# More places for loaded weights and words, loads later in a queue, evictions on ScalarE, splits one a step

## The chip, the cores and the metric

The kernel runs on one core of a Trainium2 chip. The metric is the device time of one execution in microseconds; the kernel before was timed in three runs.

## The reference

Three layers follow each other. (1) Attention over 2 batches, 8 heads, 768 positions and 64 columns a head, each query seeing 4 sink positions and a window of 128. (2) A mixture of 8 experts over the resulting 1536 x 512 rows: each token takes the best two of noisy logits, and the expert is relu(x w1) w2 with 1024 hidden columns. (3) A dense layer with 2048 hidden columns, whose weights come as float64:

```python
    top2 = np.argpartition(-noisy_logits, 2, axis=1)[:, :2]
    ...
            h = np.maximum(x[mask] @ w1[e], 0.0)
            out[mask] += top2_w[mask, k, None] * (h @ w2[e])
...
    h = x @ w_in
    g = h * (1.0 / (1.0 + np.exp(-h)))
    return (g @ w_out).astype(np.float32)
```

## The kernel before

Every float32 product is made from float16 halves: a high half (ScalarE, a scaled copy or relu) and a low half (VectorE, the value less the high half; `low`, line 126, and `low_relu`, line 131, which also sum what they write). A product is three matmuls: high by high, and twice high by low. The low half of h is needed by the second of the three.

The work runs in three stages: attention (to about 153 us; its end already does a part of expert 0), the experts (`moe`, to about 455 us), the dense layer (`moe2`). Each engine takes its instructions in the order of the program, which is written by hand.

*Experts.* There are 64 steps i = 8e + f (expert e, block f of 128 hidden columns). A step first does `l1(e, f)` (line 995: 12 matmuls over 416 columns, then relu on ScalarE and the low half on VectorE) and then `l2` of the step before (line 1011: 12 matmuls into four PSUM tiles `py`). In expert 0 the first 128 rows are done already, so its matmuls have 288 columns. After that, in this order in a step:

- at f = 0, `y_ev`: the four finished `py` tiles of the expert before are copied to `yT`, two by ScalarE (line 1033), two by VectorE (line 1035);
- `stores`: the store of an output tile evicted a step earlier, on SyncE;
- at f = 2 to 5, `y_pe` transposes a part of `yT` on TensorE (line 1040) and `y_store` copies it from PSUM to a tile `yo`, on ScalarE for even parts (line 1050), on VectorE for odd ones (line 1052);
- `gather`: GpSimd collects the rows of expert e + 2 at f = 5;
- `x_pair` splits gathered rows of the next expert into halves (high, line 974, ScalarE; low, VectorE) in a tile `rows`, and `x_turn` transposes them into `xT` by a transposing DMA on SyncE (line 1351). Both take two of the four parts in a step: in expert 0 splits at f = 3 and 4 and turns at f = 5 and 6, later splits at f = 1 and 2 and turns at f = 3 and 4. Experts alternate between `rows[0]` and `rows[1]`;
- `weights_step(k)`: piece k of the weights is split (high half, line 871, ScalarE; low, VectorE), then SyncE loads piece k + 3 (line 866). Each piece is 512 KB in a place of the pool `wst`, which has three, so that load waits for the low half of piece k. There is one piece a step, and two in a few steps from i = 10 on;
- `decode_step`, five in four steps: the float64 weights of the dense layer become float32 by bit operations, 32 blocks of 128 x 512. An even decode step ends block n - 1 (`a4`: line 939 on VectorE, and either a split into halves, line 945 on ScalarE and a low half on VectorE, for the 16 later blocks, or a store by SyncE, line 950, for the 16 earlier ones), begins block n (`a1`: absolute value of the high words, line 924 on VectorE, then a scaling on GpSimd, line 926) and loads the words of block n + 1 (line 920, two places `f64`). An odd step does two word operations (`a2`, `a3`, lines 930 and 934, VectorE).

*Dense layer.* It begins with the gathers of the y rows of two experts a token (`gather_y`), their weighted sum and their transposes; then ScalarE's queue issues the first three loads of `late` weight pieces, and 48 steps of `l1` (line 1256) and `l2` (line 1273) follow.

Of the kernel before, what the change touches and what calls it, by code (L numbers as in the profile page):

```python
# [8 lines left out]
F32 = mybir.dt.float32  # L9
F32R = mybir.dt.float32r  # L10
F16 = mybir.dt.float16
# [811 lines left out]
class Weights:  # L823


    def __init__(self, ctx, tc, g):
        self.tc, self.g = tc, g
        self.pools = [ctx.enter_context(tc.tile_pool(name="wA", bufs=2))]
        self.stage = ctx.enter_context(tc.tile_pool(name="wst", bufs=3))
        self.u = {}  # L830

    def second(self, ctx):
        self.pools.append(ctx.enter_context(self.tc.tile_pool(name="wB", bufs=2)))
        self.own = ctx.enter_context(self.tc.tile_pool(name="wC", bufs=2))

    def src(self, u, k, h):
        g = self.g
# [18 lines left out]
    def piece(self, u, k, h, late=False):  # L856

        nc = self.tc.nc
        g = self.g
        st = {}  # L860

        def load(eng=nc.sync):
            if u not in self.u:
                self.start(u)
            st["t"] = t = self.stage.tile([128, 2, 512], F32, name="wst")
            eng.dma_start(t, self.src(u, k, h))

        scale = ((SW1, SW2), (SWI, SWO))[u >= 16][k]

        def hi():  # L870
            nc.scalar.activation(self.u[u][k][0][:, 2 * h:2 * h + 2, :], st["t"], AF.Copy, scale=scale)  # L871

        def lo():
            a, b = self.u[u][k]
            low(nc, g, b[:, 2 * h:2 * h + 2, :], st["t"], scale, a[:, 2 * h:2 * h + 2, :])
            if h == 0:
                seen(self.tc, g, a[:, 0, 0:64])

        def scaled(x):
            nc.gpsimd.tensor_scalar(st["t"][:, x], st["t"][:, x], scale, 1.0, op0=OP.mult, op1=OP.mult)  # L880

        def hi_pool(x):
            nc.gpsimd.tensor_scalar(self.u[u][k][0][:, 2 * h + x, :], st["t"][:, x], 1.0, 1.0, op0=OP.mult, op1=OP.mult)

        def lo_pool(x):
            a, b = self.u[u][k]
            nc.gpsimd.tensor_sub(b[:, 2 * h + x, :], st["t"][:, x], a[:, 2 * h + x, :])

        return load, hi, lo, hi_pool, lo_pool, scaled

    def checks(self, u, pool):

        nc = self.tc.nc
        g = self.g
        def total(x, t):
            o = pool.tile([128, 2, 512], F16, name="any", bufs=1)
            nc.scalar.activation(o, t[:, x:x + 2, :], AF.Copy, accum_out=sum_at(g))

        out = [lambda x=x, t=self.u[u][0][1]: total(x, t) for x in (0, 2)]
        return out + [lambda t=self.u[u][k][0]: seen(self.tc, g, t[:, 0, 0:64]) for k in range(2)]  # L900
# [5 lines left out]
def decode(tc, g, pool, W=None):  # L906

    nc = tc.nc
    V = nc.vector
    out = []  # L910
    for q in (2, 3, 0, 1):
        for src, dst in ((g.w_in, g.win_d), (g.w_out, g.wout_d)):
            w = src.bitcast(I32)
            for x in range(4):
                r, c = (128 * x, 512 * q) if dst is g.win_d else (512 * q + 128 * x, 0)
                st = {}

                def load(eng=nc.sync, st=st, w=w, r=r, c=c):
                    st["w"] = t = pool.tile([128, 512, 2], I32, name="f64", bufs=2)
                    eng.dma_start(t, w[r:r + 128, 2 * c:2 * c + 1024].rearrange("p (f w) -> p f w", w=2))  # L920

                def a1(st=st):
                    st["a"] = a = pool.tile([128, 512], F32, name="f32", bufs=2)
                    V.tensor_scalar(a.bitcast(I32), st["w"][:, :, 1], 0x7fffffff, None, op0=OP.bitwise_and)  # L924

                    nc.gpsimd.tensor_scalar(a, a, 2.0 ** -15, 2.0 ** -80, op0=OP.max, op1=OP.mult)  # L926

                def a2(st=st):
                    l = st["w"][:, :, 0]
                    V.tensor_scalar(l, l, 29, -0x80000000, op0=OP.logical_shift_right, op1=OP.bitwise_or)  # L930

                def a3(st=st):
                    l = st["w"][:, :, 0]
                    V.scalar_tensor_tensor(l, st["w"][:, :, 1], -0x80000000, l, op0=OP.bitwise_and,
                                           op1=OP.bitwise_xor)

                def a4(st=st, dst=dst, r=r, c=c, q=q, x=x):
                    a = st["a"].bitcast(I32)
                    V.scalar_tensor_tensor(a, a, 3, st["w"][:, :, 0], op0=OP.logical_shift_left,  # L939
                                           op1=OP.bitwise_xor)  # L940
                    if W and q < 2:
                        k = int(dst is g.wout_d)
                        hi, lo = (t[:, x, :] for t in W.u[16 + q][k])
                        scale = (SWI, SWO)[k]
                        nc.scalar.activation(hi, st["a"], AF.Copy, scale=scale)  # L945
                        low(nc, g, lo, st["a"], scale, hi)
                        if x == 0:
                            seen(tc, g, hi[:, 0:64])
                    else:
                        nc.sync.dma_start(dst[r:r + 128, c:c + 512], st["a"])  # L950

                out.append((load, a1, a2, a3, a4))
    return out


def moe(tc, g, W, wk, ps):
# [72 lines left out]
    def y_ev(e, d):  # L1029
        if d == 0:  # L1030
            yT[e] = wk.tile([128, 4, 512], F32, name="yT", bufs=1)[:, :, :C]
        if d % 2 == 0:
            nc.scalar.activation(yT[e][:, d, part(e)], ys[e][d][:, part(e)], AF.Copy)
        else:
            V.tensor_copy(yT[e][:, d, part(e)], ys[e][d][:, part(e)])

    def y_pe(e, c):
        t = tp[c] = ps.tile([128, 4, 128], F32, name="tpy", tag="PT")
# [6 lines left out]
    def y_store(e, c, src):  # L1045
        t = wk.tile([128, 512], F32, name="yo", bufs=2)
        n = CT[c]
        src = src[:n]
        if c % 2 == 0:
            nc.scalar.activation(t[:n], src, AF.Copy)  # L1050
        else:
            V.tensor_copy(t[:n], src)
        return lambda: nc.sync.dma_start(g.y_d[e * C + c * 128:e * C + c * 128 + n, :], t[:n])
# [45 lines left out]
            loaded[0] += 1  # L1099

    xT[0] = g.xT
    load_ahead(3)
    seq = [(e, f) for e in range(E) for f in range(8)]

    small, stores = [], []
# [1 line left out]
    def weights_step(k):  # L1107
        if k < len(todo):
            todo[k][1]()
            todo[k][2]()  # L1110
            load_ahead(k + 4)

    def decode_step(i):
        n, odd = divmod(i, 2)
        if i > 64:
            return
        if odd:
            dec[n][2]()
            dec[n][3]()
        else:  # L1120
            if n > 0:
                dec[n - 1][4]()
            if n < len(dec):
                dec[n][1]()
                if n + 1 < len(dec):
                    dec[n + 1][0]()

    dstep = [0]
    done = [0]
    for i, (e, f) in enumerate(seq):  # L1130
        l1(e, f)
# [16 lines left out]
        if f == 5 and e + 2 < E:  # L1148
            gather(e + 2)
        if e + 1 < E:  # L1150
            z = 2 * (f - (1 if e else 3))
            for c in (z, z + 1):
                if 0 <= c < 4:
                    x_pair(e + 1, c)
            for c in (z - 4, z - 3):
                if 0 <= c < 4:
                    x_turn(e + 1, c)
        if i == 1:
            small.extend(W.checks(0, wk) + W.checks(1, wk))

# [10 lines left out]
            g.pre()  # L1171
        if i == 7:
            dec[0][0]()
        if i < 9:
            continue
        decode_step(dstep[0])
# [12 lines left out]


def gather_y(tc, g, pool, j, k):
    t = g.yy[j, k] = pool.tile([128, 512], F32, name=("yg", "xg")[k], bufs=4)
    rows = (g.E - 1) * g.C
    if k:
        rows = rows + g.CY if j < 4 else g.E * g.C
    tc.nc.gpsimd.indirect_dma_start(
        out=t, out_offset=None, in_=g.y_d[:rows, :],
        in_offset=bass.IndirectOffsetOnAxis(ap=g.slot[:, j, k:k + 1], axis=0))


def moe2(tc, g, W, wk, ps):
# [92 lines left out]
        x_pe(j, ("M", "PT")[j // 2])  # L1294
        x_ev(j)
    g.rest()
    for p in late[:3]:
        p[0](nc.scalar)
    NQ = g.N // 512
    seq = [(q, f) for q in range(NQ) for f in range(16)]  # L1300
    for i, (q, f) in enumerate(seq):
# [6 lines left out]
        if i < len(late):  # L1308
            late[i][1]()
            late[i][2]()  # L1310
            if i + 3 < len(late):
                late[i + 3][0]()
        if q + 1 < NQ:
            j = 4 * (q + 1)
            for stage, f0 in ((lambda j: (gather_y(tc, g, wk, j, 0), gather_y(tc, g, wk, j, 1)), 2),
# [9 lines left out]
def fast(ctx, tc, g):  # L1325
# [17 lines left out]

    def pair_rows(e, c):

        t = g.rows[e % 2][:, c, :].bitcast(F16)
        return t[:, 0:512], t[:, 512:1024]

    def turn(xT, e, c, n):

        tc.nc.sync.dma_start_transpose(xT[2][:, :, 128 * c:128 * c + n], g.rows[e % 2][:n, c, :].bitcast(F16))

    g.xT_tiles, g.pair_rows, g.turn = xT_tiles, pair_rows, turn
    g.rows = [early.tile([128, 4, 512], F32, name=f"rows{x}") for x in range(2)]
# [67 lines left out]
def general(tc, g):  # L1422
# [4 lines left out]
    with ExitStack() as ctx:  # L1427
# [131 lines left out]
        with ExitStack() as st:  # L1559
            wk = st.enter_context(tc.tile_pool(name="gend", bufs=1))  # L1560
            for stages in decode(tc, g, wk):
                for f in stages:
                    f()

        with ExitStack() as st:
            wk = st.enter_context(tc.tile_pool(name="genc", bufs=1))
# [72 lines left out]
```

## Time and profile before

| | us |
|---|---|
| median of three runs | 722.78 |
| lowest and highest run | 721.03, 723.17 |
| profiled execution, its own time | 721.78 |
| its span in the profile | 720.1 |
| TensorE busy | 668.8 (93%) |
| VectorE busy | 444.0 (62%) |
| ScalarE busy | 313.1 (43%) |
| GpSimd busy | 204.5 (28%) |

The busy shares are means over the three stages, which differ. In the rows below PE is TensorE's matmuls, DVE VectorE, ACT ScalarE, SPq and ACTq the queues in which SyncE and ScalarE issue DMAs. "<-" behind a time in square brackets names what ended an engine's idle time.

### The profile page before, as it was taken

Reading aid. Unit: us, or ns where it says so; the run is one execution under the profiler, and the core shown is the slowest. Engines: PE = TensorE matmul, PEld = TensorE weight load, DVE = VectorE, ACT = ScalarE, POOL = GpSimd, SP = SyncE. Lnnn points to the kernel's source line nnn. Section 1 sums busy time; section 2 is a strip of 40 time slices with the busy share of each in tenths; the row PEclk is TensorE's granted clock in tenths of the full one; section 3 lists DMA queues with packets and bytes.
Section 4 is the critical chain, followed back from the end, with each engine's and each line's share of the span. In section 5 each row is a group of like instructions: output and inputs, shape, how many; then the busy total and the mean of one; then the engine's idle time right before and its main releaser. Section 6 shows DMA issues by size and latency. Waiting matters only on the chain.

```text
span 720.1 us, 11583 instructions
## 1 busy us (share of the span) xinstructions
PE 668.8 (93%) x4292; PEld 373.1 (52%) x4292; DVE 444.0 (62%) x1137; ACT 313.1 (43%) x647; POOL 204.5 (28%) x229
## 2 busy tenths in 40 slices
PE   7999899887888999999999999899999999999994
PEld 4777677455454555555555554344444444444441
DVE  5878888736587879697989863656433343322232
ACT  4887878346544444333545331344222222222221
POOL 5868951122125252434262323231100000000000
PEclk9999999899899999999999999999999999999998
DMA  7876610338598898979595723662311011010001
GB/s 151 198 163 176 178 46 30 118 96 211 177 275 324 224 368 200 340 218 338 180 323 170 203 88 106 180 219 76 85 45 59 1 30 30 5 54 1 1 0 64
DMA packets 111681, 103.49 MB, mean 144 GB/s; under 512 B 77312, under 2 KB 77568, under 8 KB 111616
## 3 DMA queue, kind: packets, MB, share of 16 engines
q1 hardware_dynamic: 106560, 87.72, 42.4%
q0 software_dynamic: 4096, 13.11, 5.8%
q10 hardware_dynamic: 960, 1.84, 0.8%
q8 instruction: 35, 0.57, 0.3%
q14 instruction: 30, 0.25, 0.1%
HBM read 77.29 MB, written 17.30 MB: 131 GB/s over the span
## 4 chain that ended last, share of the span: by engine, by line


## 5 line engine op out<-in xcount | busy, mean ns | idle before, releaser
L995 PE MATMUL ph<-xT,w 128*128 128x416 f16 (+1 forms) x768 | 141.6, 335 | 8.3 <-DMA xT<-rows 6.4
L1011 PE MATMUL py<-h,w 128*128 128x416 f16 (+1 forms) x672 | 126.7, 334 | 12.3 <-DVE h L131 11.7
L1256 PE MATMUL p<-xT,w 128*128 128x512 f16 x576 | 132.1, 379 | 2.1 <-DVE xT L1242 1.4
L1273 PE MATMUL po<-w,h 128*128 128x512 f16 x576 | 132.1, 379 | 0.0
L926 POOL TENSOR_SCALAR f<-f 128x512 f32<-128x512 f32 x32 | 65.0, 2032 | 168.9 <-DVE f L924 161.8
L995 PEld LDWEIGHTS <-w 128*128 128x128 f16 x768 | 75.4, 98 | 60.7 <-DMA xT<-rows 6.6
L1259 DVE TENSOR_TENSOR f<-p,f 128x512 f32<-128x512 f32 x48 | 33.1, 690 | 110.9 <-ACT f L1258 110.9
L1011 PEld LDWEIGHTS <-w 128*128 128x128 f16 x672 | 66.1, 98 | 63.9 <-issue 18.4
L1256 PEld LDWEIGHTS <-w 128*128 128x128 f16 x576 | 56.3, 98 | 70.1 <-issue 2.4
L1273 PEld LDWEIGHTS <-h 128*128 128x128 f16 x576 | 56.2, 98 | 67.8 <-DVE h L126 0.3
L126 DVE SCALAR_TENSOR_TENSOR w<-wst,w 128x1024 f16<-128x1024 f32 x64 | 79.1, 1238 | 15.8 <-ACT w L871 13.4
L1258 ACT ACTIVATE f<-p 128x512 f32<-128x512 f32 x48 | 28.6, 596 | 129.2 <-PE p L1256 127.9
L871 ACT ACTIVATE w<-wst 128x1024 f16<-128x1024 f32 x64 | 66.9, 1047 | 12.0 <-DMA wst<-in_moe_w_dram 12.0
L998 ACT ACTIVATE h<-ph 128x416 f16<-128x416 f32 (+1 forms) x64 | 31.8, 497 | 78.1 <-PE ph L995 75.1
L126 DVE SCALAR_TENSOR_TENSOR h<-f,h 128x512 f16<-128x512 f32 x48 | 33.2, 692 | 33.3 <-ACT h L1261 32.6
L131 DVE SCALAR_TENSOR_TENSOR h<-ph,h 128x416 f16<-128x416 f32 (+1 forms) x64 | 36.3, 566 | 19.9 <-ACT h L998 19.9
L1261 ACT ACTIVATE h<-f 128x512 f16<-128x512 f32 x48 | 30.2, 629 | 37.8 <-DVE f L1259 37.0
L482 ACT ACTIVATE P<-pS,mx 128x260 f32<-128x260 f32 (+1 forms) x96 | 43.0, 458 | 0.5 <-DVE mx L473 0.2
L966 POOL DMA_INDIRECT xg<-x_d,idx x28 | 29.7, 1059 | 23.2 <-DVE topsl L121 13.4
L504 DVE SCALAR_TENSOR_TENSOR plo<-pPT,phi 128x512 f16<-128x512 f32 (+1 forms) x48 | 30.5, 636 | 4.1 <-ACT phi L499 4.1
L945 ACT ACTIVATE w<-f 128x512 f16<-128x512 f32 x16 | 10.1, 630 | 51.7 <-DVE f L939 51.7
L473 DVE TENSOR_REDUCE mx<-pS 128x2 f32<-128x520 f32 (+1 forms) x48 | 31.0, 646 | 1.4 <-PE pS L467 1.2
(252 smaller groups left out, 886.3 us busy)
## 6 DMA issues: line engine op xcount, KB each, us to landing
wst<-in_moe_w_dram SPq DMA_DIRECT2D x64, 512.0 KB
f<-in_moe_w_in_dram SPq DMA_DIRECT2D x16, 512.0 KB
f<-in_moe_w_out_dram SPq DMA_DIRECT2D x16, 512.0 KB
y_d<-yo SPq DMA_DIRECT2D x23, 256.0 KB
rawv<-in_v_dram SPq DMA_DIRECT2D x12, 256.0 KB
x_d<-xs SPq DMA_DIRECT2D x12, 256.0 KB
rows<-in_k_dram SPq DMA_DIRECT2D x11, 256.0 KB
rows<-in_q_dram SPq DMA_DIRECT2D x11, 256.0 KB
```

Of the source, the lines that this page charges most:

```text
L126: nc.vector.scalar_tensor_tensor(o, x, scale, hi, op0=OP.mult, op1=OP.subtract, accum_out=sum_at(g)[:o.shape[0]] if check else None)
L131: nc.vector.scalar_tensor_tensor(o, x, 0.0, hi, op0=OP.max, op1=OP.subtract, accum_out=sum_at(g))
L473: nc.vector.tensor_reduce(t, psS[pr][:, :, :wd], axis=AX.X, op=OP.max, negate=True)
L482: nc.scalar.activation(Pt[n][:, h, :wd], psS[pr][:, a, :wd], AF.Exp, bias=nmx[pr][:, a:a + 1], accum_out=sm[n][:, h:h + 1])
L871: nc.scalar.activation(self.u[u][k][0][:, 2 * h:2 * h + 2, :], st["t"], AF.Copy, scale=scale)
L926: nc.gpsimd.tensor_scalar(a, a, 2.0 ** -15, 2.0 ** -80, op0=OP.max, op1=OP.mult)
L995: nc.tensor.matmul(p[:, v], w[x][:, d, c], xT[e][y][:, d, v], start=d == 0 and k == 0, stop=d == 3 and k == 2)
L998: nc.scalar.activation(hi[:, v], p[:, v], AF.Relu)
L1011: nc.tensor.matmul(ys[e][d][:, v], w[x][:, f % 4, d * 128:(d + 1) * 128], h[y][:, v], start=f == 0 and k == 0, stop=f == 7 and k == 2)
L1256: nc.tensor.matmul(p, w[x][:, d, c], xT[q][y][:, d, :], start=z == 0, stop=z == 11)
L1259: V.tensor_mul(s, p, s)
L1273: nc.tensor.matmul(po[q][t], h[x][:, 128 * t:128 * t + 128], w[y][:, f % 4, :], start=f == 0 and k == 0, stop=f == 15 and k == 2)
```

## The change

- The weight places become five for the pieces from the second expert on: the three of `wst` and two made of `rows[1]`, which is therefore no longer used for split rows: all experts split into `rows[0]`. SyncE loads piece k + 4 after piece k is split; five are loaded ahead instead of three, also at the start of the dense layer, where ScalarE's queue issues them.
- The words have four places `f64`, and an even decode step loads block n + 2. The store of decoded words is issued in the next odd decode step. The first gathered rows of the dense layer take their places among the `f64` tiles.
- The absolute value (`a1`) is an activation Abs of ScalarE that reads the high words as float32.
- All four `y_ev`, and all `y_store` of the experts before the last, are on ScalarE.
- `x_pair` takes one part a step at f = 1 to 4, `x_turn` one at f = 2 to 5, for every expert.
- Scratch output of `checks` goes to `yo` tiles.

```diff
@@ Weights
-        self.stage = ctx.enter_context(tc.tile_pool(name="wst", bufs=3))
+        self.stages = [ctx.enter_context(tc.tile_pool(name="wst", bufs=3))]
+        self.turn = 0
...
-            st["t"] = t = self.stage.tile([128, 2, 512], F32, name="wst")
+            z = self.turn
+            if z < 3:
+                t = self.stages[0].tile([128, 2, 512], F32, name="wst")
+            elif z < 5:
+                t = g.rows[1][:, 2 * z - 6:2 * z - 4, :]
...
+            self.turn = (z + 1) % (3 if u < 2 else 5)
@@ checks
-            o = pool.tile([128, 2, 512], F16, name="any", bufs=1)
+            o = pool.tile([128, 512], F32, name="yo", bufs=2).bitcast(F16)
@@ decode
-                    st["w"] = t = pool.tile([128, 512, 2], I32, name="f64", bufs=2)
+                    st["w"] = t = pool.tile([128, 512, 2], I32, name="f64", bufs=4)
...
-                    V.tensor_scalar(a.bitcast(I32), st["w"][:, :, 1], 0x7fffffff, None, op0=OP.bitwise_and)
+                    nc.scalar.activation(a, st["w"][:, :, 1].bitcast(F32), AF.Abs)
...
-                        nc.sync.dma_start(dst[r:r + 128, c:c + 512], st["a"])
+                        return lambda: nc.sync.dma_start(dst[r:r + 128, c:c + 512], st["a"])
@@ moe
-        if d % 2 == 0:
-            nc.scalar.activation(yT[e][:, d, part(e)], ys[e][d][:, part(e)], AF.Copy)
-        else:
-            V.tensor_copy(yT[e][:, d, part(e)], ys[e][d][:, part(e)])
+        nc.scalar.activation(yT[e][:, d, part(e)], ys[e][d][:, part(e)], AF.Copy)
...
-        if c % 2 == 0:
+        if c % 2 == 0 or e < E - 1:
...
-    load_ahead(3)
+    load_ahead(5)
...
-            load_ahead(k + 4)
+            load_ahead(k + 5)
...
         if odd:
+            while dstore:
+                dstore.pop()()
             dec[n][2]()
             dec[n][3]()
         else:
             if n > 0:
-                dec[n - 1][4]()
+                dstore.extend(f for f in [dec[n - 1][4]()] if f)
             if n < len(dec):
                 dec[n][1]()
-                if n + 1 < len(dec):
-                    dec[n + 1][0]()
+                if n + 2 < len(dec):
+                    dec[n + 2][0]()
...
-            z = 2 * (f - (1 if e else 3))
-            for c in (z, z + 1):
-                if 0 <= c < 4:
-                    x_pair(e + 1, c)
-            for c in (z - 4, z - 3):
-                if 0 <= c < 4:
-                    x_turn(e + 1, c)
+            if 0 <= f - 1 < 4:
+                x_pair(e + 1, f - 1)
+            if 0 <= f - 2 < 4:
+                x_turn(e + 1, f - 2)
...
             dec[0][0]()
+            dec[1][0]()
@@ gather_y
-    t = g.yy[j, k] = pool.tile([128, 512], F32, name=("yg", "xg")[k], bufs=4)
+    if k:
+        t = pool.tile([128, 512], F32, name="xg", bufs=4)
+    else:
+        t = pool.tile([128, 512, 2], I32, name="f64", bufs=4).rearrange("p f w -> p (f w)").bitcast(F32)[:, 0:512]
+    g.yy[j, k] = t
@@ moe2
-    for p in late[:3]:
+    for p in late[:5]:
...
-            if i + 3 < len(late):
-                late[i + 3][0]()
+            if i + 5 < len(late):
+                late[i + 5][0]()
@@ fast
-        t = g.rows[e % 2][:, c, :].bitcast(F16)
+        t = g.rows[0][:, c, :].bitcast(F16)
...
-        tc.nc.sync.dma_start_transpose(xT[2][:, :, 128 * c:128 * c + n], g.rows[e % 2][:n, c, :].bitcast(F16))
+        tc.nc.sync.dma_start_transpose(xT[2][:, :, 128 * c:128 * c + n], g.rows[0][:n, c, :].bitcast(F16))
```

## Rows read from the trace of the kernel before

**Rows 1.** TensorE's waits over the span: line, releaser, us in total, times, longest.
```profile
PE py L1011 <- DVE h L131: 11.7, 12, 2.8
PE ph L995 <- DMA xT<-rows: 6.4, 1, 6.4
```

**Rows 2.** Timeline of TensorE: start us, us, instruction, [idle before].
```profile
182.44 3.72 PE L995 MATMUL ph<-xT,w 128*128 128x416 f16 x12 [6.36 <-DMA xT<-rows]
...
191.69 2.27 PE L995 MATMUL ph<-xT,w 128*128 128x416 f16 x12
...
195.91 2.27 PE L995 MATMUL ph<-xT,w 128*128 128x416 f16 x12
...
200.56 2.27 PE L995 MATMUL ph<-xT,w 128*128 128x416 f16 x12
...
214.56 2.09 PE L1011 MATMUL py<-h,w 128*128 128x416 f16 x11 [1.71 <-DVE h L131]
...
230.26 3.52 PE L1011 MATMUL py<-h,w 128*128 128x416 f16 x11 [2.75 <-DVE h L131]
```

**Rows 3.** Busy us by stretch, experts 3 and 6: length, engines, clock, DMA share, GB/s.
```profile
260.94:298.69 37.75, 35.98 (x209) 20.56 (x208) 29.57 (x69) 15.87 (x24) 14.62 (x10) 1.00 0.93 271
...
374.78:412.15 37.37, 36.15 (x210) 20.55 (x208) 33.35 (x82) 16.57 (x28) 12.44 (x7) 1.00 0.70 213
```

**Rows 4.** VectorE's waits from 337 to 412 us.
```profile
DVE w L126 <- ACT w L945: 7.0, 10, 0.7
```

**Rows 5.** SyncE's queue, its waits from 183 to 440 us.
```profile
SPq L866 <- DVE w L126: 88.8, 25, 7.8
```

**Rows 6.** Groups by line, 187 to 440 us: busy us, mean ns | idle before, releasers.
```profile
L126 DVE SCALAR_TENSOR_TENSOR w<-wst,w 128x1024 f16<-128x1024 f32 x49 | 60.8, 1243 | 6.0 <-ACT w L871 6.0
L871 ACT ACTIVATE w<-wst 128x1024 f16<-128x1024 f32 x49 | 51.3, 1049 | 9.2 <-DMA wst<-in_moe_w_dram 9.2
L131 DVE SCALAR_TENSOR_TENSOR h<-ph,h 128x416 f16<-128x416 f32 x55 | 32.1, 583 | 12.3 <-ACT h L998 12.3
L998 ACT ACTIVATE h<-ph 128x416 f16<-128x416 f32 x54 | 27.5, 510 | 61.2 <-PE ph L995 58.2 <-issue 3.0
L939 DVE SCALAR_TENSOR_TENSOR f<-f,f 128x512 int32<-128x512 int32 x32 | 21.9, 685 | 1.8 <-POOL f L926 1.6
L924 DVE TENSOR_SCALAR f<-f 128x512 int32<-128x512 int32 x32 | 13.5, 423 | 17.9 <-DMA f<-in_moe_w_out_dram 13.1 <-DMA f<-in_moe_w_in_dram 4.9
L945 ACT ACTIVATE w<-f 128x512 f16<-128x512 f32 x16 | 10.1, 630 | 51.7 <-DVE f L939 51.7
L1052 DVE COPY yo<-tpy 128x512 f32<-128x512 f32 (+1 forms) x14 | 9.5, 680 | 0.6 <-PE tpy L1040 0.6
L1050 ACT ACTIVATE yo<-tpy 128x512 f32<-128x512 f32 x13 | 7.7, 594 | 16.7 <-PE tpy L1040 14.3 <-DMA y_d<-yo 2.4
L1035 DVE COPY yT<-py 128x416 f32<-128x416 f32 (+1 forms) x14 | 7.3, 562 | 0.0
L1065 ACT ACT_TABLE_LOAD x1 | 1.3, 1283 | 0.0
```

**Rows 7.** Timeline of VectorE in expert 0's step 4 and in expert 2's first steps.
```profile
169.12 0.68 DVE L126 SCALAR_TENSOR_TENSOR rows<-xg,rows 32x512 f16<-32x512 f32 x1
...
229.28 0.43 DVE L924 TENSOR_SCALAR f<-f 128x512 int32<-128x512 int32 x1 [3.73 <-DMA f<-in_moe_w_out_dram]
```

**Rows 8.** Timeline of SyncE's queue at the end of expert 0.
```profile
177.26 0.52 SPq L866 DMA_DIRECT2D wst<-in_moe_w_dram  x1
177.83 2.58 SPq L1351 DMA_TRANSPOSE xT<-rows  x2
```

**Rows 9.** Timeline of ScalarE and its queue at the dense layer's start.
```profile
458.73 1.92 ACTq L866 DMA_DIRECT2D wst<-win_d  x1
...
460.69 0.48 ACTq L866 DMA_DIRECT2D wst<-wout_d  x1
...
463.30 0.60 ACT L1258 ACTIVATE f<-p 128x512 f32<-128x512 f32 x1 [0.81 <-PE p L1256]
```

More of the change, by code (lines that the diff above doesn't have):

```diff
@@ L864, in load @@
                 self.start(u)
-            st["t"] = t = self.stage.tile([128, 2, 512], F32, name="wst")
+            z = self.turn
[4 more added lines that the diff above has]
+            else:
+                t = self.stages[1].tile([128, 2, 512], F32, name="wst")
+            st["t"] = t
+            self.turn = (z + 1) % (3 if u < 2 else 5)
             eng.dma_start(t, self.src(u, k, h))
@@ L895, in total @@
         def total(x, t):
-            o = pool.tile([128, 2, 512], F16, name="any", bufs=1)
-            nc.scalar.activation(o, t[:, x:x + 2, :], AF.Copy, accum_out=sum_at(g))
+            o = pool.tile([128, 512], F32, name="yo", bufs=2).bitcast(F16)
+            nc.scalar.activation(o.rearrange("p (a b) -> p a b", a=2), t[:, x:x + 2, :], AF.Copy, accum_out=sum_at(g))
         out = [lambda x=x, t=self.u[u][0][1]: total(x, t) for x in (0, 2)]
@@ L1121, in decode_step @@
             if n > 0:
-                dec[n - 1][4]()
+                dstore.extend(f for f in [dec[n - 1][4]()] if f)
             if n < len(dec):
                 dec[n][1]()
-                if n + 1 < len(dec):
-                    dec[n + 1][0]()
-    dstep = [0]
+                if n + 2 < len(dec):
+                    dec[n + 2][0]()
+    dstep, dstore = [0], []
     done = [0]
@@ L1191, in gather_y @@
 def gather_y(tc, g, pool, j, k):
-    t = g.yy[j, k] = pool.tile([128, 512], F32, name=("yg", "xg")[k], bufs=4)
+    if k:
+        t = pool.tile([128, 512], F32, name="xg", bufs=4)
+    else:
+        t = pool.tile([128, 512, 2], I32, name="f64", bufs=4).rearrange("p f w -> p (f w)").bitcast(F32)[:, 0:512]
+    g.yy[j, k] = t
     rows = (g.E - 1) * g.C
@@ L1562, in general @@
                 for f in stages:
-                    f()
+                    store = f()
+                store()
         with ExitStack() as st:
```

## The prediction

> **What bounds the kernel now.** I read the page's busy shares first: TensorE is busy 93% of 720.1 us, so only what stands between its matmuls can be won. Then the waits of TensorE over the whole span [rows 1]: two entries belong to the expert stage, 11.7 us in twelve waits of the second product for the low half of h, written by VectorE, and one wait of 6.4 us of the first product for xT, written by transposing DMAs. All other entries lie in attention or at the start of the last stage, where the change hardly reaches.
>
> Then TensorE's timeline gives a floor [rows 2]. A step (l1 of one block, l2 of the block before) takes 195.91 - 191.69 = 4.22 us, a step with a y_pe in it 200.56 - 195.91 = 4.65 us. An expert of eight steps, four with y_pe, is 4 x 4.22 + 4 x 4.65 = 35.5 us. Expert 1 has three y_pe and a shorter l2 (288 columns, some 0.6 us less): 34.5 us. Experts 1 to 6 should take 34.5 + 5 x 35.5 = 212.0 us and run from 182.44 [rows 2] to 412.15 [rows 3], 229.7 us: 17.7 us too many. The 6.4 us before expert 1 come on top. So **24.1 us** is all that the change can give back here. Part of it is slower matmuls behind the two longest gaps: twelve of l1 after the 6.36 us took 3.72 us instead of 2.27, and eleven of l2 after the 2.75 us took 3.52 instead of 2.09 [rows 2].
>
> What makes the low half late? In the late experts VectorE itself: it was busy 33.35 of 37.37 us in expert 6 [rows 3], and over the two experts from 337 to 412 it waited 7.0 us, ten times 0.7, for ScalarE's high half of decoded weights [rows 4]. 33.35 + 3.5 = 36.9 us: VectorE is the bound there, not TensorE. In the earlier experts it is the order of SyncE's queue: SyncE stood 88.8 us before weight loads whose place was not yet free [rows 5], everything behind came late, and ScalarE then waited 9.2 us for weights and VectorE 17.9 us for float64 words [rows 6]. The 2.75 us gap is such a case: VectorE stood 3.73 us before the first operation on a late word tile, and the low half of h was queued behind it [rows 7].
>
> **The change part by part.**
>
> *Splits spread over steps (x_pair at f = 1 to 4, x_turn at f = 2 to 5) with five places.* For expert 1 the last low half of a row split ended near 169.8 in step 4 [rows 7], but its transposes were the last two of SyncE, issued at 177.83, behind a weight load at 177.26 that waited for a place [rows 8]; xT came at 182.44 while TensorE was ready at 182.44 - 6.36 = 176.1. The last split stays in step 4. With five places a load waits for the piece before the current one, so the last turn can be issued near 170. The two turns took 2.58 us of SyncE, and the data came 2.0 us after their end (180.4). One last turn alone, issued near 170, brings xT at 173.3; if all four stood behind one another from 170, it would be 177.2, against 176.1. Bounds of what is left: 0 and 1.1 us; I take 0.5, since three turns lie in earlier steps but weight loads stand between them. Gain 5.9, and the 1.45 us of slower matmuls inside expert 1.
>
> *More places and words, later loads.* The weight loads' 88.8 us of standing still should nearly go: a load now asks for a place freed a step earlier; the word tile of block n+2 asks for one last read two decode steps back; and a store of decoded words is issued a step after its data. Decode takes a block every 1.6 steps, some 7 us (five blocks in an expert of 35.5 us), so the words are asked for 14 us ahead instead of 7 less the time SyncE stood, and the 17.9 us go; so do the gap of 2.75 us and the 1.4 us of slower matmuls behind it.
>
> *VectorE relieved.* 32 absolute values of 0.42 us (13.5 us), 14 copies of yT (7.3) and 14 copies of outputs (9.5) leave VectorE [rows 6]. In expert 6 that is 5 x 0.42 + 2 x 0.56 + 2 x 0.68 = 4.6 us: 36.9 - 4.6 = 32.3 us, under the floor of 35.5, so TensorE is the bound again. ScalarE takes them: 5 absolute values, for which the trace has no row; a plain SBUF pass over 512 columns is the nearest, 0.63 us (L945), bounds 0.42 (VectorE's price) and 1.05 (twice the columns, L871); I take 0.6. With 2 yT of 0.51 (as relu over the same 416 columns) and 2 outputs of 0.59 that makes 16.57 + 5.2 = 21.8 of 35.5 us [rows 3, 6]. Busy time is no obstacle; order is.
>
> *What stands behind the new waits.* All four y_store of an expert now sit on ScalarE in front of x_pair, of the high halves of weights and of relu of the next step, and each waits for y_pe, TensorE's last work in that step. The 13 that were there already waited 14.3 us [rows 6]. I work out step f = 3 of a late expert, from T, the start of its l1: y_pe ends at T + 4.65; output copy to 5.45; x_pair's high half to 6.05; high half of weights 1.05 to 7.05; on VectorE the low half, 1.32, to 8.4; last decode operation 0.69, 9.1; ScalarE's high half of it 0.63, 9.75; VectorE's low half 0.69, 10.45; two word operations of the next half step (0.42 and 0.69 by the nearest rows), 11.55; low half of h 0.58, 12.1. TensorE wants that at T + 4.65 + 4.65 + 2.11 + 0.17 = 11.6. Late by 0.5 (all durations [rows 6]; the 0.2 us from the end on TensorE to the start on ScalarE is an estimate); step 4, starting from that backlog, by 0.7 more in the same way. So experts 5 and 6 keep some 1.1 us each, expert 4 (half of it with such decode steps) 0.8, experts 2 and 3, where decoded words are only stored and ScalarE need not answer, 0.3 each. Bounds: 0, if the queues interleave better, and 3 us an expert.
>
> *Expert 1* keeps most of its VectorE trouble: two weight pieces a step for three steps are 2 x 1.32 us beside 0.66 for h, 0.76 for the row split (0.68 and 0.08 [rows 7]), 1.1 for decode and some small ones, near 6 us in a step of 4.65. It had a wait of 1.71 there [rows 2] and smaller ones; I leave 1.9.
>
> *The start of the last stage.* Two more loads are issued from ScalarE's queue, ahead of its first sigmoid. One issue cost 0.48 us, another 1.92; the sigmoid waited 0.81 us for TensorE [rows 9]. Cost between 0 (2 x 0.4 hidden) and 2 x 1.92 - 0.81 = 3.0 us; I take 0.5, near the 0.48 row. Behind it everything is matmul after matmul with all data early: nothing changes. Attention keeps its three places: nothing. Scratch output in "yo" and word tiles as the place of the first gathered row: both free long before, nothing.
>
> Sum left: 0.5 + 1.9 + 0.3 + 0.3 + 0.8 + 1.1 + 1.1 + 0.5 = 6.5 us. Gain 24.1 - 6.5 = 17.6 us. The profiled execution took 721.78 us (span 720.1 and 1.7 around it), 1.0 us under the median 722.78 and inside the runs (721.03 to 723.17). 721.8 - 17.6 = 704.2; against the median 705.2. I say **705 us**.
>
> **Rivals.**
>
> *A. ScalarE's order gives half of it back* (0.22). For it: the 14.3 us above and the chain through both engines. Against it: two steps of TensorE lie between relu and its use. At 2 us in each of experts 1 to 6 and 2 us at the start of the last stage, 14 of 24.1 us stay: 712 us.
>
> *B. The DMA engines are the bound* (0.07). In expert 3 their busy share was 0.93 at 271 GB/s [rows 3]: 0.93 x 37.75 = 35.1 us of work, just under the floor. If earlier loads only queue there, as much is late as before and only the boundary (7.8 us) and the late experts' half (3.8 us) are won: 711 us. The Trainium skill, "DMA: Bandwidth & Descriptors", section "Where 436 GB/s comes from", puts the limit of HBM to SBUF traffic at about 358 GB/s a core; by it expert 3's 10.2 MB would need 28.6 us (an estimate) and the rival would be far off. The share in the trace says it is near, and the share decides.
>
> *C. Slower: the output copies block ScalarE* (0.05). One mechanism: 27 output copies of experts 0 to 6 stand on ScalarE waiting for y_pe, relu of the next step comes behind a full round of both engines, and l2 waits each time. It decides from 24.1 / 27 = 0.9 us a copy; at 1.4 us it is 38 - 24 = 14 us slower, 737 us. The step above gives 0.5 to 0.7 us for two of four copies only in late experts, so it is far from that.
>
> *D. The absolute value needs its own function table* (0.01). ScalarE loaded one table among the steps from 187 on, for an Exp, 1.28 us [rows 6]; two loads for each of 5 an expert are 12.8 us, ScalarE then has 34.6 us of work in an expert and 4 x 1.3 us of waits for y_pe, 39.8 us, 1.5 us more than the 38.3 of before in each of six; with the boundary won, 725 us. The trace has no row of this function. The Trainium skill, "ScalarE: Activation LUTs", section "Table sets: the hidden batching unit", says that abs stands in every set, like copy and relu; Copy and Relu do alternate here without a load, which agrees.
>
> *E. Nothing moves* (0.03): other late data take the place of each wait; 722 us.
>
> **How the numbers follow.** The forecast holds 0.62, from 699 (all 24.1 us gone: 698.7) to 709. A and B reach to 716. Range 699 to 714 leaves out the slow half of A's upper end, C, D and E. A repeat of this kernel tells a difference of 0.3%, 2.2 us. Faster: 0.62 + 0.22 + 0.07 and a bit of E, 0.92; the same 0.03; slower 0.05.
>
> **What would show it.** TensorE's wait for xT before expert 1 under 1 us and no slowed l1 behind it; expert 6 at 35.5 to 37 us with VectorE's busy time near 29; no VectorE wait for word tiles; SyncE's wait before weight loads under 20 us; ScalarE waiting for y_pe some 27 times; the leftover waits of l2 at f = 4 and 5. Wrong: if l2's waits for h together stay over 9 us, or expert 3 stays over 37 us with a DMA share near 1.

## The result and the profile after

The changed kernel takes 713.09 us (median; 712.12 to 714.80), against 722.97 us before: ratio 0.9871, 95% interval 0.9844 to 0.9898. It is faster by 9.9 us, inside the range 699 to 714, but 8 us slower than the 705 us forecast. The profiled execution took 714.80 us (span 713.1), 7.0 us under that of before.

Lengths from the first l1 matmul of an expert to the next expert's, read off TensorE's timeline (us); the floor is the prediction's, and for expert 0, for which it gave none, seven steps of 2.94 us and one l1 of 1.47:

| kernel | expert 0 | 1 | 2 | 3 | 4 | 5 | 6 |
|---|---|---|---|---|---|---|---|
| floor | 22.0 | 34.5 | 35.5 | 35.5 | 35.5 | 35.5 | 35.5 |
| before | 29.3 | 38.4 | 40.1 | 37.8 | 38.7 | 37.4 | 37.4 |
| after | 22.0 | 36.5 | 42.7 | 36.7 | 38.5 | 37.6 | 37.8 |

The whole gain lies before expert 1. Experts 1 to 6 together take 229.8 us, as before (229.7). The rest of the 7.0 us is small: attention ended 1.5 us earlier, and what follows expert 6 took 1.6 us longer, 1.1 of it behind the last matmul; the kernels below began their experts anywhere between 151.2 and 154.3 us, so I read nothing into the first of these.

The lines have moved: 995 (l1) is 1006, 1011 (l2) 1022, 998 (relu) 1009, 871 and 866 (weights) 882 and 877, 924 (absolute value) 936, 939 and 945 (end of a decoded block, its high half) 950 and 956, 950 (store of decoded words) 961, 1033 (yT) 1043, 1050 (output copy) 1058, 1351 (turn) 1363.

TensorE's waits over the span of the changed kernel, to be held against [rows 1]:

```profile
PE py L1022 <- ACT h L1009: 4.0, 2, 3.8
PE py L1022 <- DVE h L131: 3.8, 8, 0.6
PE py L1022 <- ACT yT L1043: 2.4, 4, 1.3
...
PE ph L1006 <- DMA xT<-rows: 1.2, 1, 1.2
```

The 6.4 us for xT before expert 1 are gone (the 1.2 left stand before expert 2), and the waits for VectorE's low half fell from 11.7 to 3.8 us. Two new entries name ScalarE: relu itself was late (3.8 us in one place), and the copies of yT. The place of the long one, on TensorE (first fence), ScalarE (second) and SyncE's queue (third):

```profile
210.28 2.27 PE L1006 MATMUL ph<-xT,w 128*128 128x416 f16 x12 [1.23 <-DMA xT<-rows]
216.39 4.61 PE L1022 MATMUL py<-h,w 128*128 128x416 f16 x12 [3.84 <-ACT h L1009]
220.79 3.16 PE L1006 MATMUL ph<-xT,w 128*128 128x416 f16 x12
```

```profile
202.92 1.05 ACT L882 ACTIVATE w<-rows 128x1024 f16<-128x1024 f32 x1
215.27 0.66 ACT L936 ACTIVATE f<-f 128x512 f32<-128x512 f32 x1 [11.30 <-DMA win_d<-f]
215.83 0.51 ACT L1009 ACTIVATE h<-ph 128x416 f16<-128x416 f32 x1
...
220.61 0.66 ACT L936 ACTIVATE f<-f 128x512 f32<-128x512 f32 x1 [3.33 <-DMA win_d<-f]
```

```profile
203.97 0.71 SPq L961 DMA_DIRECT2D win_d<-f  x1
...
209.87 0.33 SPq L961 DMA_DIRECT2D win_d<-f  x1
```

ScalarE stood 11.30 us before an absolute value, that of the fourth block. It writes a tile `f32`, of which there are two, and the block two before, the second, had the same tile; its store to `win_d` had to be finished first. That store is the second one of SyncE, issued at 203.97; the absolute value began 11.3 us later. The third store, issued at 209.87, ended the next such wait in the same way (220.61, 10.7 us later). Relu stood behind the absolute value. TensorE lost 3.84 us and, with the slower matmuls behind the gap (4.61 and 3.16 instead of 2.27 each), 3.2 more; the granted clock from 215 to 221 us, just behind that stand, was 0.56, near the lower of its two levels (1.2 of 2.4 GHz). Over experts 1 to 6 ScalarE's waits are these (175 to 404 us: total, times, longest):

```profile
ACT w L956 <- DVE f L950: 34.1, 12, 3.6
ACT yo L1058 <- PE tpy L1048: 21.3, 12, 2.8
ACT f L936 <- DMA win_d<-f: 16.6, 4, 11.3
ACT f L936 <- DMA wout_d<-f: 11.6, 3, 4.4
```

28.2 us stand before stores. ScalarE's wait for weights is gone, and nothing waits for words any more, as the groups of lines show (175 to 403 us; the answer to [rows 6]):

```profile
L882 ACT ACTIVATE w<-wst 128x1024 f16<-128x1024 f32 x30 | 31.4, 1053 | 0.0
...
L936 ACT ACTIVATE f<-f 128x512 f32<-128x512 f32 x29 | 19.4, 667 | 34.2 <-DMA win_d<-f 16.6 <-DMA wout_d<-f 11.6 <-issue 6.0
```

Experts 2, 3 and 6 by engine (columns as in [rows 3]):

```profile
210.28:252.96 42.68, 38.71 (x208) 21.43 (x208) 26.82 (x66) 21.41 (x36) 15.82 (x10) 0.92 0.89 289
252.96:289.63 36.67, 35.88 (x210) 20.57 (x209) 26.27 (x61) 19.05 (x31) 14.45 (x9) 1.00 0.94 274
365.78:403.58 37.80, 36.23 (x209) 20.54 (x208) 29.18 (x72) 22.48 (x39) 11.12 (x7) 1.00 0.60 188
```

In expert 6 VectorE is busy 29.18 us instead of 33.35, ScalarE 22.48 instead of 16.57, and the expert is no shorter.

### The profile page after: what moved, and what is told of

It is laid out like the page before. It is cut to its first block, busy times and chain, and to the rows that moved or that the text cites. A ratio compares the mean times of both kernels' runs of the same rounds, so it can differ in the third digit from the quotient of the medians.

```text
span 713.1 us, 11614 instructions
## 1 busy us (share of the span) xinstructions
PE 668.9 (94%) x4292; PEld 372.9 (52%) x4292; DVE 418.7 (59%) x1077; ACT 341.7 (48%) x707; POOL 209.4 (29%) x229
## 4 chain that ended last, share of the span: by engine, by line
## 5 line engine op out<-in xcount | busy, mean ns | idle before, releaser
L1022 PEld LDWEIGHTS <-w 128*128 128x128 f16 x672 | 66.1, 98 | 62.2 <-issue 16.8
L126 DVE SCALAR_TENSOR_TENSOR w<-wst,w 128x1024 f16<-128x1024 f32 x38 | 46.3, 1221 | 15.9 <-ACT w L882 15.9
L882 ACT ACTIVATE w<-wst 128x1024 f16<-128x1024 f32 x38 | 39.7, 1051 | 0.0
L126 DVE SCALAR_TENSOR_TENSOR w<-rows,w 128x1024 f16<-128x1024 f32 x26 | 31.6, 1220 | 11.5 <-ACT w L882 11.4
L977 POOL DMA_INDIRECT xg<-x_d,idx x28 | 32.7, 1166 | 19.4 <-DVE topsl L121 12.4
L936 ACT ACTIVATE f<-f 128x512 f32<-128x512 f32 x32 | 21.3, 667 | 34.2 <-DMA win_d<-f 16.6
```

Of the source, the lines that this page charges most:

```text
L126: nc.vector.scalar_tensor_tensor(o, x, scale, hi, op0=OP.mult, op1=OP.subtract, accum_out=sum_at(g)[:o.shape[0]] if check else None)
L977: nc.gpsimd.indirect_dma_start(out=t[:CT[c]], out_offset=None, in_=g.x_d[:, :], in_offset=bass.IndirectOffsetOnAxis(ap=g.idx[:CT[c], 4 * e ...
L1022: nc.tensor.matmul(ys[e][d][:, v], w[x][:, f % 4, d * 128:(d + 1) * 128], h[y][:, v], start=f == 0 and k == 0, stop=f == 7 and k == 2)
```

## The experiments

All ratios are to the kernel before. "Changed" is the changed kernel; "three f32" is the changed kernel with three tiles `f32`, on which later ones build.

| kernel | median us | ratio, 95% interval |
|---|---|---|
| changed | 713.1 | 0.9871 [0.9844, 0.9898] |
| changed, stores at once | 709.8 | 0.9819 [0.9778, 0.9860] |
| changed, three f32 | 704.9 | 0.9751 [0.9711, 0.9792] |
| changed, absolute values on VectorE | 709.5 | 0.9826 [0.9785, 0.9867] |
| changed, yT split over two engines | 712.0 | 0.9845 [0.9798, 0.9892] |
| before, splits one a step alone | 710.6 | 0.9856 [0.9820, 0.9892] |
| changed, old splits | 719.8 | 0.9952 [0.9931, 0.9974] |
| three f32, three weight places | 712.1 | 0.9866 [0.9817, 0.9914] |
| three f32, halves later | 700.2 | 0.9697 [0.9664, 0.9729] |
| three f32, copies last | 700.1 | 0.9690 [0.9654, 0.9727] |
| three f32, both | 699.9 | 0.9669 [0.9631, 0.9707] |
| three f32, both, yT split | 698.5 | 0.9667 [0.9637, 0.9697] |

**Stores at once.**

```diff
-            while dstore:
-                dstore.pop()()
...
-                dstore.extend(f for f in [dec[n - 1][4]()] if f)
+                f = dec[n - 1][4]()
+                if f:
+                    f()
```

> The changed kernel with one part undone: the store of decoded words is issued in its own decode step again, not in the next one. Store theory (ScalarE stands 28 us before Abs until the store of the block that had the same f32 tile has landed, and relu stands behind Abs): the longest of these waits, 11.3 us before expert 2, falls under 5 us, expert 2 goes from 42.7 to under 39 us, the whole to about 708 us. Queue theory (the DMA queue is simply fuller, whatever is issued lands late): SyncE now stands before the store instead, later loads come late, 713 us within 2.

ScalarE's waits for stores fell from 28.2 to 15.7 us and expert 2 from 42.7 to 37.5, as the store theory had it, but the longest only from 11.3 to 8.5 us, where under 5 was expected: a store issued at once is still waited for. Something of the queue theory holds too: TensorE's waits for xT rose from 1.2 to 4.7 us, and expert 3, which ends in one of them, took 39.9 instead of 36.7 us. The whole is 3 us faster, its interval overlapping that of the changed kernel. ScalarE from 172 to 405 us, and TensorE from 150 to 470:

```profile
ACT f L936 <- DMA win_d<-f: 9.0, 2, 8.5
ACT f L936 <- DMA wout_d<-f: 6.7, 1, 6.7
```

```profile
PE ph L1006 <- DMA xT<-rows: 4.7, 2, 2.6
```

**Three f32.**

```diff
-                    st["a"] = a = pool.tile([128, 512], F32, name="f32", bufs=2)
+                    st["a"] = a = pool.tile([128, 512], F32, name="f32", bufs=3)
...
```

> The changed kernel with three places instead of two for the tile f32 that Abs writes. Store theory: the store that Abs waits for is then one block (some 7 us) older, ScalarE's waits for stores fall from 28 us to under 5, experts 2 to 4 go from 117.9 us together to about 110, the whole to about 705 us. Queue theory: the waits move to words, weights or xT, the whole stays at 711 to 714 us.

(The dense layer's tiles of that name get three places too.) This settles what the wait is worth: 704.9 us, and experts 2, 3 and 4 take 35.9, 35.5 and 35.5 us, the floor within 0.4. Two waits for stores are left (7.3 and 0.6 us, expected under 5 in all). The long one falls together with a wait of TensorE for xT, 2.3 us before expert 2 (expert 1 takes 37.7 us), and costs little beside it. ScalarE from 175 to 396 us, and expert 3 by engine:

```profile
ACT f L936 <- DMA win_d<-f: 7.3, 1, 7.3
...
ACT f L936 <- DMA wout_d<-f: 0.6, 1, 0.6
```

```profile
248.98:284.49 35.51, 35.51 (x209) 20.58 (x208) 26.78 (x62) 21.36 (x34) 15.64 (x10) 1.00 0.99 308
```

**Absolute values on VectorE.**

```diff
-                    nc.scalar.activation(a, st["w"][:, :, 1].bitcast(F32), AF.Abs)
+                    V.tensor_scalar(a.bitcast(I32), st["w"][:, :, 1], 0x7fffffff, None, op0=OP.bitwise_and)
```

> The changed kernel with the absolute values back on VectorE, all else as changed. Store theory: VectorE now stands before the store in ScalarE's place, with the low half of h behind it; the gap of expert 2 stays, 713 us within 2. Rival (the engine matters: ScalarE is what is overloaded in its order): ScalarE's waits for stores vanish and VectorE hides them, 707 us. In experts 5 and 6, which store nothing, the first theory has no say; if the chain between the two engines bounds them they stay at 37.5 us within 0.7.

Between the two. The wait does move to VectorE, with a gap of 3.35 us in expert 2 (39.6 us), but it is shorter, and experts 1 and 3 come to 35.5 us each. Experts 5 and 6, without stores, took 37.3 and 37.6 us. VectorE from 172 to 405 us:

```profile
DVE f L936 <- DMA win_d<-f: 7.1, 3, 3.4
DVE f L936 <- DMA wout_d<-f: 5.7, 2, 3.3
```

**yT split.**

```diff
-        nc.scalar.activation(yT[e][:, d, part(e)], ys[e][d][:, part(e)], AF.Copy)
+        if d % 2 == 0:
+            nc.scalar.activation(yT[e][:, d, part(e)], ys[e][d][:, part(e)], AF.Copy)
+        else:
+            V.tensor_copy(yT[e][:, d, part(e)], ys[e][d][:, part(e)])
```

> The changed kernel with two of the four yT copies of each expert back on VectorE. TensorE waited 2.4 us in four times for yT from ScalarE. If it is only ScalarE's load at f = 0 that counts, these waits go and 2 to 3 us are won, 710 us. If the chain of ScalarE and VectorE together bounds the experts, what yT loses the low half of h gains (VectorE takes 1.1 us an expert more), and the whole stays at 713 us within 1.5.

The time can't be told from the changed kernel's. The waits for yT stayed (2.9 us in four), those for the low half went from 3.8 to 1.1; experts 5 and 6 took 37.0 and 37.2 us.

**Splits alone, in the kernel before; and the reverse, old splits in the changed kernel.**

```diff
-            z = 2 * (f - (1 if e else 3))
...
-                    x_turn(e + 1, c)
+            if 0 <= f - 1 < 4:
+                x_pair(e + 1, f - 1)
+            if 0 <= f - 2 < 4:
+                x_turn(e + 1, f - 2)
```

> The kernel before with one part of the change alone: splits one a step at f = 1 to 4, turns one a step at f = 2 to 5, with three places for weights and everything else as before. If the order of splits and turns is what gave the boundary, TensorE's wait for xT before expert 1 falls from 6.4 us to under 2, some 7 us are won, 716 us. If it needs the five places too (a turn stands behind a load whose place is not free), 3 to 5 us of the wait stay, 719 to 721 us.

> The changed kernel with one part undone: splits and turns two a step as before, in rows[0] for all experts, all other parts as changed. If the spread of splits is what the whole gain of 10 us came from (alone in the kernel before it gave 11), the boundary of expert 1 costs its 6 us again and the whole is 719 to 724 us, no gain. If five places and free turns get xT there in time without it, the boundary stays closed and it is 712 to 715 us.

Both come out for the spread of splits. Alone it gives 11 us, as much as the whole change (the intervals overlap): expert 0 falls from 29.3 to 23.9 us, and experts 1 to 6 from 229.7 to 223.0, which I had not expected. Without it the other parts give 3.5 us (0.48% by the ratio); expert 0 then takes 25.7 us, 3.7 over its floor where some 6 were expected, and experts 1 to 6 take 229.5, as with it. TensorE's waits with the splits alone, 150 to 400 us:

```profile
PE py L1011 <- DVE h L131: 7.1, 10, 3.0
PE ph L995 <- DMA xT<-rows: 1.8, 2, 1.6
```

With old splits in the changed kernel SyncE's queue shows what the places can't help: the last two turns are again issued late, in step 6:

```profile
167.61 4.47 SPq L1366 DMA_TRANSPOSE xT<-rows  x2
...
172.76 2.59 SPq L1366 DMA_TRANSPOSE xT<-rows  x2
```

**Three weight places** (with three f32).

```diff
-            self.turn = (z + 1) % (3 if u < 2 else 5)
+            self.turn = (z + 1) % 3
-    load_ahead(5)
+    load_ahead(3)
...
-            load_ahead(k + 5)
+            load_ahead(k + 4)
...
```

> The changed kernel with three f32 tiles, and with three weight places and the old look-ahead (three, and k + 4) instead of five. If the places are what keeps ScalarE and VectorE supplied, ScalarE waits for weights again (9 us before), SyncE stands 60 us or more before loads, and 704.9 becomes 709 or more. If words and stores were the only late data, it stays at 705 us within 1.5.

7 us slower than with five: the places do keep something. (The dense layer goes back to three loads ahead as well; the loss lies before it, 1.4 us in expert 0 and 5.9 in experts 1 to 6.) Less at the weights themselves (ScalarE waited 4.1 us for them) than at other transfers: ScalarE's waits for stores rose from 7.9 to 12.7 us, and TensorE waited for xT in three experts. TensorE from 150 to 470 us:

```profile
PE ph L1006 <- DMA xT<-rows: 6.1, 3, 2.9
```

**Halves later, and copies last** (each with three f32).

```diff
+                        def halves():
+                            nc.scalar.activation(hi, st["a"], AF.Copy, scale=scale)
+                            low(nc, g, lo, st["a"], scale, hi)
...
+                        return halves
...
```

```diff
             y_pe(e - 1, f - 2)
-            y_out(e - 1, f - 2)
...
             decode_step(dstep[0])
             dstep[0] += 1
+        if e > 0 and 2 + (e == 1) <= f < 6:
+            y_out(e - 1, f - 2)
```

> The changed kernel with three f32 tiles, and the two halves of a decoded block (ScalarE, then VectorE) put off from the even decode step that ends the block to the odd one behind it. Loop theory (in experts 5 and 6 ScalarE stands 28.6 us before VectorE's last decode operation with relu queued behind it, and VectorE then stands before ScalarE: a chain with no slack, 37.6 us an expert): the waits go, experts 5 and 6 fall to 36.3 us or less, the whole from 704.9 to about 702 us. Rival (output copies in front of the queue, waiting for y_pe, are what holds relu): nothing changes, 705 us within 1.

> The changed kernel with three f32 tiles, and the output copy of a step at the end of ScalarE's work for the step instead of ahead of the splits. If the copies in front, which stood 21 us before y_pe, hold relu up, experts 5 and 6 fall from 37.6 to 36.5 us or less, VectorE's waits for the high halves of weights fall from 23 us by half, and the whole to about 702 us. Loop theory: experts 5 and 6 stay at 37.6 within 0.4, 705 us within 1.

They give 4.7 and 4.8 us by the medians, some 4 by the ratios, so both remedies work, and each theory was wrong to deny the other's any effect. Halves later: experts 5 and 6 from 37.6 and 37.8 to 36.3 and 36.1 us, as expected. Copies last: 36.0 and 37.3, where 36.5 or less was expected of both. In both kernels expert 1 takes 36.0 instead of 37.7 us; no halves of decoded blocks are made there, so with halves later this part of the gain is not that edit's, and I credit it to neither. ScalarE's wait for VectorE's last decode operation, over the last experts with three f32 (320 to 395 us), with halves later (317 to 389) and with copies last (318 to 392):

```profile
ACT w L956 <- DVE f L950: 28.6, 10, 3.6
```

```profile
ACT w L958 <- DVE f L950: 3.5, 2, 1.7
```

```profile
ACT w L956 <- DVE f L950: 29.7, 10, 3.6
```

Copies last leaves that wait and still gains. What it takes away is ScalarE's wait for y_pe, from 20.8 to 5.4 us between 172 and 405 us; VectorE's waits for the high halves of weights, which it was to halve, fell only from 23.1 to 19.5. That the two are links of one chain is an argument from these waits.

**Both, and both with yT split.**

> The changed kernel with three f32 tiles, halves of decoded blocks a half step later and output copies last in a step. If the two remedies take away different waits, experts 2 to 6 all stand at the floor of 35.5 us within 0.4 and the whole comes to about 698 us. If both cut the same chain, it stays at 700 us within 1.

> As the kernel with both remedies, and two of four yT copies back on VectorE. If TensorE still waits for yT or for the low half at f = 1 and 2, 0.5 us an expert more is won, 696 us. If VectorE and ScalarE both have slack by then, nothing changes: the same as the kernel with both remedies within 1 us.

In both, experts 2 to 6 stand at 35.5 us each. In time the two (699.9 and 698.5 us) and their parts (700) can hardly be told apart, though 698 us was expected of both if the remedies took away different waits. With yT split expert 1 takes 35.0 us and expert 0 22.5; it has the lowest median here, 2.1% faster than the changed one by the two ratios. TensorE's waits in it from 150 to 390 us, and expert 6 by engine:

```profile
PE ph L1010 <- ACT Aoh L704: 1.8, 1, 1.8
PE ph L1010 <- issue: 0.3, 1, 0.3
PE ph L1010 <- DMA xT<-rows: 0.2, 1, 0.2
```

```profile
351.74:387.25 35.51, 35.51 (x210) 20.58 (x208) 29.95 (x74) 21.11 (x36) 12.70 (x6) 1.00 0.66 185
```

## Why the prediction was right or wrong

**The floor was right.** 35.5 us an expert and 24.1 us to be won: the last kernel reaches 35.5 in five experts, and its experts 0 to 6 take 235.0 us, 23.9 less than before.

**The time lies in the range by its width.** Of the 12.2 us forecast to be won in experts 1 to 6 (17.7 less the 5.5 left there) none came; the whole gain is expert 0's, and the result stands 0.9 us inside the upper end. Of the signs named, expert 6 at 35.5 to 37 us failed (37.8).

**The boundary was right**, and better than forecast: no wait before expert 1, where 0.5 us had been left. The last turn went out at 167.1, not near 170:

```profile
167.08 1.18 SPq L1363 DMA_TRANSPOSE xT<-rows  x1
```

What I missed is that the same edit alone takes 6.7 us out of experts 1 to 6 of the kernel before; the prediction had credited it there with 1.45, the slower matmuls in expert 1. No run tells how the rest comes about, and in the changed kernel, with its waits for stores, undoing the edit costs those experts nothing.

**The step that failed**: what the absolute value must wait for once ScalarE does it. The prediction books it with 0.6 us of busy time ("Busy time is no obstacle; order is") and books "a store of decoded words is issued a step after its data" only as relief of the queue. I did not ask who waits for the store. The tile that it reads is written again two blocks later, by an instruction that the change had just put in front of relu. Priced 0; measured 28.2 us of ScalarE's time and, by the run with three f32, some 8 us of the whole. Expert 2, forecast with 0.3 us over the floor, had 7.2. Putting the store off is the smaller part: the stores behind the two waits at the start of expert 2 were issued 1.9 and 1.8 us after their data and were waited for until 11.3 and 10.7 us after their issue, and with stores at once only 3 us were won.

Before the change there were two such tiles as well, but no wait named a store, and SyncE's queue shows why. The words of the block that writes the tile next were issued behind that store, and it was for these words that VectorE stood until 229.28 [rows 7]. With the words loaded earlier the store is what comes last:

```profile
220.64 0.34 SPq L950 DMA_DIRECT2D win_d<-f  x1
221.02 0.43 SPq L920 DMA_DIRECT2D f<-in_moe_w_out_dram  x1
```

**The late experts**: 1.1 us over the floor forecast for 5 and 6, 2.1 and 2.3 measured. The chain worked out there (output copy, splits, weights, last decode operation, halves, relu) is the one at which the two remedies work, each at another link; with both, these experts are at the floor. The size was off by two. "VectorE is the bound there" was too simple: taking 4.2 us of work from it won nothing, because its waits for ScalarE grew as much, from 7.0 us over experts 5 and 6 [rows 4] to 16.8 (328 to 403 us):

```profile
DVE w L126 <- ACT w L956: 7.6, 11, 0.7
DVE w L126 <- ACT w L882: 6.5, 8, 1.8
DVE h L131 <- ACT h L1009: 1.9, 7, 0.3
DVE rows L126 <- ACT rows L985: 0.8, 2, 0.4
```

**Expert 1** had 1.9 us left in the forecast and 2.0 in the run, by luck: the forecast put them down to VectorE, and the run has 1.23 us of waiting for xT before expert 2, which no term foresaw, and one wait of 0.28 us for the low half.

**The start of the dense layer**: 0.5 us forecast; five loads took ScalarE's queue from 449.2 to 453.9, the sigmoid came late, and l2 lost 0.55 us of waiting and 0.3 of slower matmuls:

```profile
453.93 1.28 ACT L1270 ACT_TABLE_LOAD   x1 [4.16 <-issue]
455.22 0.60 ACT L1270 ACTIVATE f<-p 128x512 f32<-128x512 f32 x1
```

```profile
457.26 3.07 PE L1285 MATMUL po<-w,h 128*128 128x512 f16 x12 [0.55 <-ACT h L1273]
```

**The rivals.** A has the time (712 us), nearer than the forecast, but only part of the cause: ScalarE's order does give back what was won, mostly through a wait that A did not name. B fell as the bound: in expert 3 of the kernel with three f32 TensorE stands at its floor with the same transfers, at a share of 0.99. It has a part all the same, since the late stores and the late xT of expert 2 are transfers of a stretch, expert 1, in which the share rose from 0.83 to 0.95. C did not come: the copies waited 21.3 us and cost at most the 4.8 that copies last gave. D fell: the absolute value took 0.667 us (0.6 taken), and no table was loaded for it: between 175 and 403 us ScalarE loads one, for the Exp, as before. The Trainium skill, "ScalarE: Activation LUTs", section "Table sets: the hidden batching unit", counts abs among the cheap functions that every set holds, and the trace agrees. The forecast sign that SyncE would stand under 20 us before weight loads was a bad one: over all releasers it stood some 90 us there from 175 to 402 us (112 before, from 183 to 440), with weights and words early all the same.

## What to carry to other kernels

When a store reads a tile that is written again, look for the next writer of that tile and for what is queued behind that writer on its engine, and count until the store has landed, not until it is issued. A third buffer was worth 8 us here, while two parts of the moved work (the absolute values, half of the yT copies) could be moved back, with two buffers, without any loss. When two in-order engines feed each other, neither is the bound by its busy time: cut the chain by moving one link a half step, and only then move work. Test the smallest edit of a bundle alone: one of six gave as much as all six together.

## What the runs showed that I had not expected

How long a transfer takes to land. In the changed kernel the store issued at 196.23 was waited for until 200.0, 3.8 us later, the one of 203.97 until 215.27, 11.3 us later. Where the trace gives a time to landing, the longest is 9.3 us for weights and 11.5 for words; with the splits alone in the kernel before, where fewer loads are issued ahead, it is 7.4 and 7.7. That the loads issued ahead hold up the stores fits these numbers, but with three weight places, where the longest is 8.1 and 8.9, ScalarE waited longer for stores (12.7 us, with five 7.9), so it is not shown. SyncE issued the store of 209.87 late by 1.5 us that the trace puts down to the landing of an output store; why it should wait for that one no run tells.
